# A two-mixer kernel with half of the second mixer's up and down weights decoded in the second mixer's first block

## The chip, the cores and the metric

The kernel runs on one core of a Trainium2 chip. The metric is the time of one execution on the device in microseconds (us). The engines are named as in the profile: PE (TensorE, matmuls), PEld (its weight loads), DVE (VectorE), ACT (ScalarE), POOL (GpSimd) and SP (SyncE, which issues every DMA here).

## The reference, cut to what matters

The inputs are r, k and v (4 batches, 8 heads, 768 positions, 48 channels each), the decay w and the bonus u, and the weights of two mixers. Three layers follow one another:

```python
# 1: a linear attention with a state that decays
cur = einsum('bhd,bhe->bhde', u * k[t], v[t])
y[t] = einsum('bhd,bhde->bhe', r[t], state + cur)
state = w * state + einsum('bhd,bhe->bhde', k[t], v[t])
# 2: mixer 1 (384 -> 1024 -> 384) with a convolution over 3 positions
h = maximum(x @ w_in, 0)
x = (h * sigmoid(conv3(h, conv_w))) @ w_out
# 3: mixer 2 (384 -> 1536 -> 384) with a layer norm
xn = (x - mean) / sqrt(var + 1e-6) * g_ln
out = x + maximum(xn @ w_ch1, 0) @ w_ch2
```

The weights reach the kernel as 64-bit floating-point numbers, two 32-bit words each. The kernel turns them into 32-bit numbers itself, and splits every number into a high part and a low part, so that a product is three matmuls (high by high, high by low, low by high).

## The kernel before, in words

**Tiles and blocks.** The positions are cut into 24 tiles of 128 for the attention and into 8 blocks of 384 (three tiles) for the mixers. `attn_tile` (L237) and `state_update` (L310) make one tile in two steps of the generator `attention` (L331); `step()` runs one such step. Mixer 1 (`mixer1`) runs over 8 slices f of its hidden width per block. For each f, `moe1_up` (L385) makes nine matmuls into `psm`, DVE and ACT apply the convolution and the gate (L376, L377, L382, L383, L393, L394, L396), and `down` makes nine matmuls into `acc`, two to three slices later (`LAG` is 3). Mixer 2 (`mixer2`) runs over 12 slices per block in the same way; its `moe2_up` (L402) has only one ACT operation (L409) and one DVE operation (L410) per slice. `norm` prepares the next block's normalised input. All of mixer 1's blocks, with the attention between their slices, come before all of mixer 2's blocks; the blocks' results go through DRAM in between.

**The weights.** Every weight matrix is decoded in pieces. A piece (a "job", `wjob`, L126) is one DMA into one of three buffers `st` and a generator of steps: the absolute value (ACT), a clamp, a shift and two combining operations (DVE), the high part (ACT) and the low part (DVE). A piece takes four calls of the generator, and the low part falls to the fifth, which goes on to the next piece. There are 22 pieces, in the order of `wjobs`: three of the first half of `w_in` (512 wide; all later ones but the next three of `w_in` are 768 wide), one of `w_out`, three of the second half of `w_in`, three of `w_out`, six of `w_ch1` (three for slices 0 to 5, three for slices 6 to 11), and six of `w_ch2` (two slices each). `wload(n)` issues the DMAs of the first n pieces. `wdo(n, last)` makes n steps, none beyond the piece `last`, and issues loads ahead (L190). `need(job)` makes all steps up to the end of a piece at once.

**Where the steps are placed.** `tables()` (L571) issues the first three tiles' loads and the first three pieces' loads, tile before piece. During the first four attention tiles the loop at L673 makes two steps after each `step()`, up to the last piece of the first half of `w_in`. In mixer 1 there are two slots per slice, 16 per block, and `after1` (L690) makes steps in them by these lines:

```python
            if j == 0:
                wdo(2, wo_job[NF1 - 1])
            elif j < NB - 2:
                wdo(slot[0] % 3 == 0, c1_job[NF2 - 1])
            else:
                wdo(slot[0] % 2 == 0, c2_job[4])
```

In mixer 2, `after2` (L719) makes two steps per slice, and `before2` (L715) calls `need` for the pieces that the slice reads.

**What orders the work.** The matmuls, the weight pieces' DMAs and their ACT and DVE operations are marked to be kept in program order among themselves (`pe`, `so`, `ao`, `vo`). All other instructions are placed on their engine's queue by the tile framework's scheduler, which works from program order, dependences and its own simulated times; each queue then runs in order on the chip. PSUM has two buffers for `psm`, three for `acc` and three for the attention.

Of the kernel before, what the change touches and what calls it, by code (L numbers as in the profile page):

```python
# [16 lines left out]
DM = H * D  # L17
# [4 lines left out]
NF2 = FF2 // 128  # L22
# [6 lines left out]
NB = B * BPB  # L29
NP = H // 2  # L30
PR = 112
WN = 768
# [11 lines left out]
def body(ctx, tc, r, k, v, w, u, w_in, conv_w, w_out, g_ln, w_ch1, w_ch2, out):  # L44
# [81 lines left out]
    def wjob(src, n, hi, lo, scale=None):  # L126

        st = []

        def load():  # L130
            st.append(io.tile([128, 2 * WN], I32, tag="st", name="st", bufs=3))
            dst = st[0][:, 0:2 * n]
            if len(src.shape) == 3:
                dst = dst.rearrange("p (a n) -> p a n", a=src.shape[1])
            so.dma_start(out=dst, in_=src.bitcast(I32))

        def steps():
            t = yield from decode(st[0], n)
            if len(src.shape) == 3:
                t = t.rearrange("p (a n) -> p a n", a=src.shape[1])  # L140
            kw = {} if scale is None else {"scale": gl[:, scale:scale + 1]}
            ao.activation(out=hi, in_=t, func=AF.Copy, **kw)
            yield
            if scale is None:
                vo.tensor_tensor(out=lo, in0=t, in1=hi.bitcast(F32), op=ALU.subtract)
            else:
                vo.scalar_tensor_tensor(out=lo, in0=t, scalar=kw["scale"], in1=hi.bitcast(F32),
                                        op0=ALU.mult, op1=ALU.subtract)
        wjobs.append((load, steps()))
        return len(wjobs) - 1  # L150
# [3 lines left out]
    def rows2(w_, f):  # L154
        return w_[f * 128:f * 128 + 256, :].rearrange("(a p) d -> p a d", p=128)
# [14 lines left out]
    for f0 in range(0, FF2, WN):  # L170
        for kt in range(KT):
            for f in range(f0 // 128, (f0 + WN) // 128):
                c1_job[f] = len(wjobs)
            wjob(w_ch1[kt * 128:kt * 128 + 128, f0:f0 + WN], WN, c1h[f0 // WN][kt],
                  c1l[f0 // WN][kt], kt)
    for f in range(0, NF2, 2):
        c2_job[f] = c2_job[f + 1] = wjob(rows2(w_ch2, f), 2 * DM, c2h[f // 2], c2l[f // 2])
    w_loaded, w_done = [0], [0]

    def wload(count):  # L180
# [5 lines left out]
    def wdo(count=1, last=None):  # L186

        for _ in range(count):
            while w_done[0] < (len(wjobs) if last is None else last + 1):
                wload(w_done[0] + 2)  # L190
                if next(wjobs[w_done[0]][1], "end") != "end":
                    break
                w_done[0] += 1
# [8 lines left out]
    def load_tile(n):  # L202
        if n >= NT:
            return
        b, i = divmod(n, TPB)
        sl = slice(i * C, i * C + C)
        rt = rbuf[n % 3]
        kt = io.tile([128, H, D], F32, tag="k", name="kt", bufs=3)
        vt = vbuf[n % 3]
        nc.sync.dma_start(out=kt, in_=k[b, :, sl, :].rearrange("h t d -> t h d"))  # L210
        nc.sync.dma_start(out=rt[:, :, 0:D], in_=r[b, :, sl, :].rearrange("h t d -> t h d"))
        nc.sync.dma_start(out=vt[:, :, 0:D], in_=v[b, :, sl, :].rearrange("h t d -> t h d"))
        loaded[n] = (rt, kt, vt)
# [359 lines left out]
    def tables():  # L573
        wc = ap.tile([PR, NP, 1], F32, tag="wc", name="wc", bufs=1)
        v_.memset(wc, 1.0)
        wv = w.rearrange("(p two) d -> two d p", two=2)
        for q in range(2):
            nc.sync.dma_start(out=wc[64 * q:64 * q + D], in_=wv[q].unsqueeze(2), allow_slow_non_contiguous=True)
        nc.sync.dma_start(out=tku[:, 1], in_=u.unsqueeze(0).to_broadcast([128, H, D]))
        load_tile(0)  # L580
        wload(1)
        load_tile(1)
        wload(2)
        load_tile(2)
        wload(3)
        nc.sync.dma_start(out=gl, in_=g_ln.rearrange("(k p) -> p k", p=128), allow_slow_non_contiguous=True)
        cst = ap.tile([128, 6 * NF1], I32, tag="cst", name="cst", bufs=1)
        cview = cst.rearrange("p (k f two) -> p k f two", k=3, two=2)
        for tap in range(3):
            nc.sync.dma_start(out=cview[:, tap], in_=conv_w[tap].bitcast(I32).rearrange("(f p two) -> p f two", p=128, two=2),  # L590
                              allow_slow_non_contiguous=True)
        make_identity(nc, ident)
        for t in rbuf + vbuf + [kks[:, 0, 0], kks[:, 1, 0]]:
            g_.memset(t[:, :, D:64], 0.0)

        pw = ap.tile([PR, NP, 8], F32, tag="pw", name="pw", bufs=1)
        ng = ap.tile([PR, NP, 8], F32, tag="ng", name="ng", bufs=1)
        tkd = ap.tile([PR, NP, C], F32, tag="t2", name="tkd", bufs=4)
        g_.memset(tr[:, :, 64:65], 1.0)
        v_.memset(tkd[:, :, 63:64], 1.0)  # L600
        v_.tensor_scalar(out=pw[:, :, 0:1], in0=wc, scalar1=DECAY_MIN, scalar2=DECAY_MAX, op0=ALU.max, op1=ALU.min)
        for e in range(1, 8):
            v_.tensor_tensor(out=pw[:, :, e:e + 1], in0=pw[:, :, e - 1:e], in1=pw[:, :, e - 1:e], op=ALU.mult)
        v_.reciprocal(out=ng, in_=pw)
        for e in range(7):
            m = 1 << e
            for eng, t, up, dn, o, top in ((v_, tkd, ng, pw, 63, 64), (g_, tr, pw, ng, 64, 63)):
                cnt = min(m, top - m + 1)
                if cnt > 0:
                    eng.tensor_tensor(out=t[:, :, o + m:o + m + cnt], in0=t[:, :, o:o + cnt],  # L610
                                      in1=up[:, :, e:e + 1].to_broadcast([PR, NP, cnt]), op=ALU.mult)
                bot = C - 1 - top
                cnt = min(m, bot - m + 1)
                if cnt > 0:
                    eng.tensor_tensor(out=t[:, :, o - m - cnt + 1:o - m + 1], in0=t[:, :, o - cnt + 1:o + 1],
                                      in1=dn[:, :, e:e + 1].to_broadcast([PR, NP, cnt]), op=ALU.mult)
        pt = ps_a.tile([128, NP, C], F32, tag="pa", name="ptk")
        for p in range(NP):
            pe.transpose(pt[:, p, 0:PR], tkd[:, p, :], ident[0:PR, 0:PR])
        for q in range(2):  # L620
            a_.activation(out=tku[:, 0].rearrange("x (p q) d -> x q p d", q=2)[:, q], in_=pt[:, :, 64 * q:64 * q + D],
                         func=AF.Copy)
        v_.tensor_copy(out=w128, in_=pw[:, :, 7:8])
        for t in sbd:
            g_.memset(t, 0.0)
        g_.memset(nhalf, -0.5)
        g_.memset(later, 1.0)
        g_.affine_select(out=later, in_=later, compare_op=ALU.is_gt, fill=0.0, base=0, pattern=[[0, NP], [1, C]],
                         channel_multiplier=-1)
        return cst  # L630
# [32 lines left out]
    def prefetch(j):  # L663
# [5 lines left out]
        return steps  # L669

    cst = tables()
    decayed_k(0)
    while finished[0] < EARLY - 1:  # L673
        step()
# [4 lines left out]
    for j in range(NB):  # L679
        slot = [0]  # L680
        while finished[0] < min((j + 1) * TT - (j % 2), NT - 1):
            step()

        def before1(f):
            if f < NF1:
                need(wi_job[f // 4])
            if f >= LAG - 1:
                need(wo_job[f - LAG + 1])

        def after1(f):  # L690
            slot[0] += 1
            pace[0] += 2 if j else 1.9
            if j == 1:
                pace[0] += 0.4
            if pace[0] >= 5:
                pace[0] -= 5
                step()
            if j == 0:
                wdo(2, wo_job[NF1 - 1])
            elif j < NB - 2:  # L700
                wdo(slot[0] % 3 == 0, c1_job[NF2 - 1])
            else:
                wdo(slot[0] % 2 == 0, c2_job[4])
            if j == NB - 1:
                if slot[0] == 1:
                    ahead[0] = prefetch(0)
                elif slot[0] >= 7:
                    next(ahead[0], None)

        mixer1(xT[j], spill(j), before1, after1)  # L710
# [3 lines left out]
    for j in range(NB):  # L714
        def before2(f):  # L715
            need(c1_job[f])
            need(c2_job[max(f - LAG + 1, 0)])

        def after2(f):  # L719
            wdo(2)  # L720
            if f == 1 and j + 1 < NB:
                ahead[0] = prefetch(j + 1)
            elif f >= 4:
                next(ahead[0], None)

        b, s0 = divmod(j, BPB)
        x1s, xn = normed.pop(j)
        mixer2(xn, lambda acc, x1s=x1s, b=b, s0=s0: finish(
            acc, x1s, lambda t0: out[b, s0 * T + t0:s0 * T + t0 + 128, :]), before2, after2)
        for _ in ahead[0]:  # L730
            pass
# [34 lines left out]
```

## Time and profile before

| what | value |
|---|---|
| three runs, median (lowest to highest) | 686.56 us (684.76 to 686.9) |
| the profiled execution's own time | 685.54 us |
| its span, first to last instruction | 683.8 us |
| mean granted share of TensorE's clock | 0.974 |
| busy: PE, PEld, DVE, ACT, POOL | 639.0, 609.8, 435.1, 270.1, 95.0 us |

The profile is of one execution. Its times begin at the span's start; 1.74 us of the profiled execution's time lie around the span. In a view of waits, a row says which engine and line waited for which, with the total, the count and the longest. In a timeline a row has its start, its duration, the engine, the line, the operation, what it writes and reads, and the idle time before it with what ended it. By the starts of L393 (64 of them) and L409 (96), mixer 1's block 0 begins at about 44.5 us, its block 1 at 104.8, block 6 at 308.6, mixer 2's block 0 at 366.0 and its block 1 at 402.8.

### The profile page before, as it was taken

Reading aid. Unit: us, or ns where it says so; the run is one execution under the profiler, and the core shown is the slowest. Engines: PE = TensorE matmul, PEld = TensorE weight load, DVE = VectorE, ACT = ScalarE, POOL = GpSimd, SP = SyncE. Lnnn points to the kernel's source line nnn. Section 1 sums busy time; section 2 is a strip of 40 time slices with the busy share of each in tenths; the row PEclk is TensorE's granted clock in tenths of the full one; section 3 lists DMA queues with packets and bytes.
Section 4 is the critical chain, followed back from the end, with each engine's and each line's share of the span. In section 5 each row is a group of like instructions: output and inputs, shape, how many; then the busy total and the mean of one; then the engine's idle time right before and its main releaser. Section 6 shows DMA issues by size and latency. Waiting matters only on the chain.

```text
span 683.8 us, 12373 instructions
## 1 busy us (share of the span) xinstructions
PE 639.0 (93%) x5100; PEld 609.8 (89%) x5100; DVE 435.1 (64%) x822; ACT 270.1 (39%) x537; POOL 95.0 (14%) x137
## 2 busy tenths in 40 slices
PE   3874799999999999999999999999999999999996
PEld 3764698889989978999999999999999999999995
DVE  5989899998988888997998524142332415242211
ACT  1336456556565565657675312122121212112110
POOL 6342032221212222200110000000000000000000
PEclk9887699999999999999999999999999999999999
DMA  8953542343324241403301002020201102020101
GB/s 180 180 133 78 154 107 72 86 104 82 94 71 95 57 119 22 140 1 114 130 36 59 23 1 70 1 70 1 70 1 36 34 1 70 1 69 1 35 1 39
DMA packets 93842, 45.15 MB, mean 66 GB/s; under 512 B 80337, under 2 KB 89682, under 8 KB 93778
## 3 DMA queue, kind: packets, MB, share of 16 engines
q1 hardware_dynamic: 93778, 44.28, 24.8%
q8 instruction: 42, 0.69, 0.4%
q14 instruction: 22, 0.18, 0.1%
HBM read 34.83 MB, written 9.44 MB: 65 GB/s over the span
## 4 chain that ended last, share of the span: by engine, by line
PE 54%; DVE 34%; ACT 5%; issue 3%; DMA 2%; POOL 1%; SPq 0%; ACTq 0%; DVEq 0%; POOLq 0%
PE acc L70 25%; PE psm L70 25%; DVE c L396 9%; DVE wdec L70 6%; DVE aT L271 3%; DVE gl L383 3%; DVE c L377 3%; DVE kks L224 2%; ACT c L376 1%; DVE rT L248 1%; DVE sn L325 1%; ACT c L394 1%; DVE xl L295 1%; PE pxt L70 1%; POOL av L256 1%
## 5 line engine op out<-in xcount | busy, mean ns | idle before, releaser
L410 DVE SCALAR_TENSOR_TENSOR rl<-psm,rh 128x384 fp32r<-128x384 f32 x96 | 53.3, 555 | 143.2 <-ACT rh L409 143.2
L409 ACT ACTIVATE rh<-psm 128x384 fp32r<-128x384 f32 x96 | 47.2, 491 | 212.2 <-PE psm L70 212.2
L70 PE MATMUL psm<-xnh,c1h 128*128 128x384 f32 x288 | 98.8, 343 | 0.0
L70 PE MATMUL psm<-xnh,c1l 128*128 128x384 f32 x288 | 97.5, 339 | 0.0
L70 PE MATMUL acc<-c2h,rh 128*128 128x384 f32 x288 | 97.2, 338 | 0.0
L70 PE MATMUL acc<-c2h,rl 128*128 128x384 f32 x288 | 97.2, 338 | 0.0
L70 PE MATMUL acc<-c2l,rh 128*128 128x384 f32 x288 | 97.1, 337 | 0.0
L70 PE MATMUL psm<-xnl,c1h 128*128 128x384 f32 x288 | 96.9, 336 | 0.0
L396 DVE SCALAR_TENSOR_TENSOR c<-h,cw,c 128x384 f32<-128x384 f32 x128 | 86.7, 681 | 12.0 <-ACT c L394 11.5
L70 PE MATMUL psm<-xh,wih 128*128 128x386 f32 x192 | 69.5, 362 | 8.2 <-ACT wih L70 4.7
L70 PE MATMUL acc<-woh,gh 128*128 128x384 f32 x192 | 68.2, 355 | 8.2 <-ACT woh L70 7.5
L70 PE MATMUL acc<-woh,gl 128*128 128x384 f32 x192 | 66.2, 345 | 2.0 <-DVE gl L383 1.9
L70 PE MATMUL acc<-wol,gh 128*128 128x384 f32 x192 | 65.9, 343 | 1.3 <-DVE wol L70 1.3
L70 PE MATMUL psm<-xl,wih 128*128 128x386 f32 x192 | 66.9, 348 | 0.0
L70 PE MATMUL psm<-xh,wil 128*128 128x386 f32 x192 | 66.7, 347 | 0.1
L433 POOL TENSOR_TENSOR rs<-rs,nhalf 128x1 f32<-128x1 f32 x24 | 15.6, 664 | 306.2 <-DVE rs L432 306.0
L70 PEld LDWEIGHTS psm<-xnl,c1h 128*128 128x128 f32 x288 | 54.3, 189 | 0.0
L70 PEld LDWEIGHTS psm<-xnh,c1h 128*128 128x128 f32 x288 | 54.3, 189 | 0.0
L70 PEld LDWEIGHTS psm<-xnh,c1l 128*128 128x128 f32 x288 | 54.2, 188 | 0.0
L70 PEld LDWEIGHTS acc<-c2l,rh 128*128 128x128 f32 x288 | 54.1, 188 | 0.0
L70 PEld LDWEIGHTS acc<-c2h,rh 128*128 128x128 f32 x288 | 54.1, 188 | 0.0
L70 PEld LDWEIGHTS acc<-c2h,rl 128*128 128x128 f32 x288 | 54.0, 188 | 0.0
(103 smaller groups left out, 1122.8 us busy)
## 6 DMA issues: line engine op xcount, KB each, us to landing
st<-in_moe_w_ch_dram SPq DMA_DIRECT2D x12, 768.0 KB, 5.3
rvbuf<-in_r_dram SPq DMA_DIRECT2D x24, 192.0 KB, 3.1
kt<-in_k_dram SPq DMA_DIRECT2D x24, 192.0 KB, 3.4
rvbuf<-in_v_dram SPq DMA_DIRECT2D x24, 192.0 KB, 3.1
x_dram<-x SPq DMA_DIRECT2D x24, 192.0 KB, 1.9
x1b<-x_dram SPq DMA_DIRECT2D x24, 192.0 KB, 2.9
out_dram<-x1b SPq DMA_DIRECT2D x24, 192.0 KB, 1.9
st<-in_moe_w_in_dram SPq DMA_DIRECT2D x6, 512.0 KB, 5.2
```

The source lines that it names most:

```text
L70: return lambda *args, **kw: tc.keep_in_program_order(op(*args, **kw))
L224: v_.tensor_tensor(out=kks[:, n % 2, :, :, 0:D], in0=loaded[n][1].unsqueeze(1).to_broadcast([128, 2, H, D]), in1=tku, op=ALU.mult)
L248: v_.tensor_tensor(out=rT, in0=prt[0:PR], in1=tr, op=ALU.mult)
L256: g_.tensor_tensor(out=av, in0=kks[:, n % 2, 1, :, 0:D], in1=rt[:, :, 0:D], op=ALU.mult)
L271: v_.copy_predicated(out=aT[:, q], mask=later.bitcast(I32), data=dps[q])
L295: v_.tensor_tensor(out=xl[:, :, sl], in0=yps, in1=xh[:, :, sl].bitcast(F32), op=ALU.subtract)
L377: v_.tensor_tensor(out=st["c"], in0=st["h"][:, 1:T + 1], in1=st["c"], op=ALU.mult)
L383: v_.tensor_tensor(out=st["gl"], in0=st["c"], in1=st["gh"].bitcast(F32), op=ALU.subtract)
L396: v_.scalar_tensor_tensor(out=c, in0=h[:, o:o + T], scalar=cw[:, tap, f:f + 1], in1=c, op0=ALU.mult, op1=ALU.add)
L409: a_.activation(out=gh, in_=ps[:, 0:T], func=AF.Relu)
L410: v_.scalar_tensor_tensor(out=gl_, in0=ps[:, 0:T], scalar=0.0, in1=gh.bitcast(F32), op0=ALU.max, op1=ALU.subtract)
L433: g_.tensor_tensor(out=rs[:, 1:2], in0=rs[:, 0:1], in1=nhalf, op=ALU.pow)
```

## The change

The pieces of `w_ch1` and `w_ch2` are put in another order: three of `w_ch1` (slices 0 to 5), three of `w_ch2` (slices 0 to 5), and then the same for slices 6 to 11. The first six of these twelve pieces are decoded in mixer 1's blocks 2 to 7 (none in block 1), the last six in mixer 2's first block, three steps per slice. Loads are issued three pieces ahead of the finished ones instead of two. The first piece's load comes right after the first tile's k, and three of its steps are made before the first `decayed_k`.

```diff
                 c1_job[f] = len(wjobs)
             wjob(w_ch1[kt * 128:kt * 128 + 128, f0:f0 + WN], WN, c1h[f0 // WN][kt],
                   c1l[f0 // WN][kt], kt)
-    for f in range(0, NF2, 2):
-        c2_job[f] = c2_job[f + 1] = wjob(rows2(w_ch2, f), 2 * DM, c2h[f // 2], c2l[f // 2])
+        for f in range(f0 // 128, (f0 + WN) // 128, 2):
+            c2_job[f] = c2_job[f + 1] = wjob(rows2(w_ch2, f), 2 * DM, c2h[f // 2], c2l[f // 2])
...
-                wload(w_done[0] + 2)
+                wload(w_done[0] + 3)
...
         nc.sync.dma_start(out=kt, in_=k[b, :, sl, :].rearrange("h t d -> t h d"))
+        if n == 0:
+            wload(1)
...
         load_tile(0)
-        wload(1)
         load_tile(1)
...
     cst = tables()
+    wdo(3)
     decayed_k(0)
...
             if j == 0:
                 wdo(2, wo_job[NF1 - 1])
-            elif j < NB - 2:
-                wdo(slot[0] % 3 == 0, c1_job[NF2 - 1])
-            else:
-                wdo(slot[0] % 2 == 0, c2_job[4])
+            elif j > 1:
+                wdo(slot[0] % 3 != 0 if j >= NB - 2 else slot[0] % 8 == 0, c2_job[NF2 // 2 - 1])
...
         def after2(f):
-            wdo(2)
+            wdo(3)
```

## Rows read from the trace of the kernel before

**Rows 1.** The page, parts 1 and 2: busy time by engine; TensorE's clock by slice.
```profile
PE 639.0 (93%) x5100; PEld 609.8 (89%) x5100; DVE 435.1 (64%) x822; ACT 270.1 (39%) x537; POOL 95.0 (14%) x137
...
PEclk9887699999999999999999999999999999999999
```
**Rows 2.** Windows by stage: length, PE, PEld, DVE, ACT, POOL busy, PEclk, DMA share, GB/s.
```profile
0.00:17.00 17.00, 6.36 (x46) 5.27 (x47) 9.24 (x33) 2.43 (x4) 11.77 (x39) 1.00 0.88 179
17.00:44.50 27.50, 21.16 (x344) 17.67 (x342) 25.52 (x45) 10.91 (x23) 12.26 (x15) 0.86 0.86 174
44.50:104.80 60.30, 45.86 (x387) 40.41 (x389) 54.81 (x91) 31.57 (x57) 11.64 (x10) 0.78 0.42 114
104.80:308.60 203.80, 199.10 (x2175) 182.77 (x2174) 184.91 (x314) 120.99 (x248) 43.70 (x50) 1.00 0.32 77
308.60:366.00 57.40, 55.43 (x360) 53.70 (x359) 51.67 (x107) 40.83 (x82) 5.75 (x6) 1.00 0.24 83
366.00:402.80 36.80, 36.80 (x215) 36.69 (x215) 21.04 (x38) 13.24 (x26) 0.00 (x0) 1.00 0.12 38
402.80:441.60 38.80, 38.80 (x227) 38.70 (x226) 13.01 (x30) 7.38 (x16) 1.65 (x3) 1.00 0.10 31
```
**Rows 3.** The same windows for decoding alone (tile wdec): length, DVE, ACT busy, PEclk, DMA.
```profile
44.50:104.80 60.30, 25.81 (x39) 10.62 (x14) 0.78 0.42 114
104.80:308.60 203.80, 24.84 (x31) 11.05 (x12) 1.00 0.32 77
308.60:366.00 57.40, 11.83 (x15) 5.21 (x6) 1.00 0.24 83
366.00:402.80 36.80, 11.83 (x15) 5.12 (x6) 1.00 0.12 38
```
**Rows 4.** PE's waits in 44.5 to 104.8 (two rows), in 104.8 to 308.6 (one).
```profile
PE acc L70 <- ACT woh L70: 7.5, 1, 7.5
PE psm L70 <- ACT wih L70: 4.7, 2, 2.5
...
PE prt L70 <- DVE aT L271: 1.5, 3, 0.7
```
**Rows 5.** Timeline of the start: first weight piece, first decayed keys, last decay table.
```profile
7.24 1.70 DVE L610 TENSOR_TENSOR tkd<-tkd,ng 112x4 f32<-112x4 f32 x7
...
8.99 1.13 SPq L70 DMA_DIRECT2D st<-in_moe_w_in_dram  x1
...
10.68 1.83 DVE L224 TENSOR_TENSOR kks<-kt,tku 128x768 f32<-128x768 f32 x2 [1.75 <-ACT tku L621]
...
19.25 0.68 ACT L70 ACTIVATE wdec<-st 128x512 f32<-128x512 f32 x1
...
19.97 1.66 DVE L70 TENSOR_SCALAR wdec<-wdec 128x512 f32<-128x512 f32 x2
...
23.26 0.67 DVE L70 SCALAR_TENSOR_TENSOR wdec<-st,wdec 128x512 int32<-128x512 int32 x1
```
**Rows 6.** SP's own waits: its weight loads behind the buffers that DVE frees.
```profile
SPq L70 <- DVE wdec L70: 26.9, 6, 9.0
```
**Rows 7.** The page, part 6: the second mixer's weight loads, median us to landing.
```profile
st<-in_moe_w_ch_dram SPq DMA_DIRECT2D x12, 768.0 KB, 5.3
```
**Rows 8.** Timelines of ACT and DVE in mixer 2's first block.
```profile
366.41 0.90 ACT L70 ACTIVATE wdec<-st 128x768 f32<-128x768 f32 x1
...
383.25 0.49 ACT L409 ACTIVATE rh<-psm 128x384 fp32r<-128x384 f32 x1 [1.14 <-PE psm L70]
...
385.34 0.96 DVE L70 TENSOR_TENSOR c2l<-wdec,c2h 128x768 fp32r<-128x768 f32 x1 [0.45 <-ACT c2h L70]
```
**Rows 9.** Lines of DVE, 366.0 to 402.8: busy, mean ns; idle before them.
```profile
L410 DVE SCALAR_TENSOR_TENSOR rl<-psm,rh 128x384 fp32r<-128x384 f32 x12 | 6.6, 551 | 9.2 <-ACT rh L409 9.2
...
L70 DVE TENSOR_TENSOR c2l<-wdec,c2h 128x768 fp32r<-128x768 f32 x3 | 2.9, 958 | 2.6 <-ACT c2h L70 2.6
```

## The prediction, made before the changed kernel was run

> **What bounds the kernel now.** I read the page's busy times first, then the granted clock by slice, then a table of windows by stage, then the same table for the decode alone, then waits and timelines where a stage loses time. The page says that PE is busy for 93% of the span, and the clock is below full speed only in the first slices [rows 1]. So the loss lies early, and the windows show where [rows 2]. From 402.8 us on, a block of mixer 2 is pure PE: 38.8 of 38.8 us busy, DVE at 13.0. Nothing can be won there but fewer matmuls. From 104.8 to 308.6 (mixer 1's blocks 1 to 5, with attention) PE is busy 199.1 of 203.8 us, DVE 184.9 of 203.8: PE bounds it and DVE stands close behind. What PE still waits for there is the end of a DVE operation (the attention mask, 1.5 us in three waits) [rows 4]. From 44.5 to 104.8 (block 0) PE is busy for 45.9 of 60.3 us at a granted clock of 0.78, DVE for 54.8: here DVE sets the pace, and PE stands still for weights that are not decoded, 7.5 us for the first down piece and 4.7 us in two waits for up pieces [rows 2, 4]. From 17 to 44.5 DVE is busy 25.5 of 27.5 us; before 17 us it is busy for only 9.2 [rows 2].
>
> **The sum** is made against the profiled execution, 685.54 us, which is 1.02 us below the median of 686.56. Each term is a difference in us.
>
> **Start: -2.0.** Three steps of the first piece move from the saturated stretch behind 17 us to a place before the first decayed keys. In the trace these are two DVE operations of together 1.66 us and one of 0.67, and 0.68 us on ACT [rows 5]; 2.3 us of DVE work. DVE has 7.8 us idle before 17 us [rows 2], of which 1.75 us lie directly before the first decayed keys, while DVE waits for ACT [rows 5]. If the weight has landed by then the work is covered, and everything behind it, which DVE paces, comes 2.3 us earlier; I take 2.0. The piece's load was issued at 8.99 us [rows 5]; right behind the first keys it goes out some 6 us earlier. Its 512 KB at 179 GB/s, the rate of that window [rows 2], hold up the loads queued behind it (the first r and v, the second tile) by 2.9 us. That is covered, since the first decayed keys wait for ACT and not for a load. If DVE's queue instead holds the clamp ahead of the keys before the piece is there, the start is late by the wait: a piece that lands at 14 us starts the keys at about 16.3 instead of 10.7, 5.6 late, of which the 2.3 us of work done come back. Ends: -5 (PE's waits in block 0 shrink too) and +5.
>
> The Trainium skill, DMA: Bandwidth & Descriptors, section on queues, rings and completion order, says that each DMA engine consumes a ring's descriptors in order, which speaks against putting a large load ahead of small urgent ones. By it this term would be as much as 2.9 us worse, -2.0 becoming about +1.
>
> **Block 0: 0.** Its 25.8 us of decode on DVE [rows 3] stay; the same two steps per slot. Its PE stalls follow DVE and shift with it. Loads come one piece earlier; they were not what PE waited for [rows 4]. Ends -5 and +3: a stall that falls differently also changes how long the clock stays low.
>
> **Blocks 1 to 5: -5.0.** Six pieces are decoded there now, 24.8 us of DVE and 11.1 of ACT [rows 3]. After the change block 1 has none and blocks 2 to 5 have two slots of sixteen each, eight steps, which is two pieces, 8.3 us. DVE is relieved of 16.6 us, from 184.9 to 168.3 of 203.8. PE can give back at most what it loses: 203.8 less 199.1 is 4.7 us [rows 2], perhaps twice that, as matmul ends are modelled. I take 5.0, since the waits named are for DVE [rows 4] and DVE then has a sixth of the time free. Ends 0 and -9.
>
> The Trainium skill, Perfetto Trace Analysis, section on the most-contended engine, judges TensorE by its weight loads and not by its matmuls. Weight loads fill 182.8 of these 203.8 us, DVE 184.9 [rows 2], so it names no clear bound; read as PE-bound throughout, it would put this term at 0 (rival 1).
>
> **Blocks 6 and 7: +1.5.** Today three pieces, 11.8 us of DVE [rows 3]. After it, two slots in three: eleven steps in block 6 and the rest of the 24 early in block 7, together sixteen steps, four pieces: 3.9 us more. DVE has 5.7 of 57.4 us idle and PE 2.0 [rows 2]. If the idle time covers it the cost is 0; if DVE is the bound it is 3.9. With 97% of DVE taken, I put it between, nearer the lower end.
>
> **Mixer 2's first block: +1.5.** Here six pieces instead of three: another 11.8 us on DVE, from 21.0 to 32.9 of 36.8 us [rows 2, 3], plus part of the second block's norm, which is now done earlier. ACT gets 5.1 more on 13.2: covered. The point is order. The seventh slice needs the second half of the up weights, three pieces. Its `rh` starts at 383.25, so its matmuls start near 381.6. In the trace three pieces begun at 366.41 end at 386.30 [rows 8], at two steps per slice. At that pace PE would stall about 3.5 us (the last third of the weights is needed near 382.8). At three steps per slice the pieces can run as fast as their chain: 3.95 us of DVE each and some 0.9 us of waiting for ACT's high part (2.6 us for three) [rows 9], with 0.7 us for the `rl` of 1.3 slices: about 5.6 us each, 16.8 in all, just in time. If all of it queues ahead of `rl` and the norm, the three pieces (11.9), seven `rl` (3.9), the waits (2.6) and 5 us of other DVE work (the window's 21.0 less 11.8 of decode and 6.6 of `rl` leave 2.6; I double it, as the second block's norm slides in) make 23.4 us against 16.8, a stall of 6.6. I take 1.5, ends 0 and +6.6. The last three pieces are needed two slices and more later and are covered.
>
> **Loads three ahead: 0.** There are three buffers, so a load now waits for the buffer of the piece just finished. SP already stands 26.9 us behind such buffers [rows 6]; queued behind it are tile loads and the blocks' stores and reloads. In mixer 2's first block a piece takes 1.3 slices, some 4.2 us, less than the 5.3 us of a load [rows 7], so two ahead would have been tight there and three cover it. No stall of PE in the trace names a load of weights.
>
> Sum: -2.0 + 0 - 5.0 + 1.5 + 1.5 = -4.0, 681.5 for the profiled execution, 682.5 against the median.
>
> **Rivals.** *1. No change* (about 686.5, 684.5 to 688.6): PE is the bound of blocks 1 to 5, its 4.7 us come back only by a fraction, and what is won there and at the start (together 3) is paid in blocks 6 and 7 and in mixer 2 (3). For it: PE at 98% in that window; against it: the waits name DVE.
>
> *2. Slower* (about 691.5): DVE comes out of block 7 with work left over, and the seventh slice of mixer 2's first block waits the full 6.6 us for its up weights. A stall of PE of that length has a second price: after the 7.5 us stall of block 0 the clock's slice falls to 0.6 [rows 1], and 17 us at 0.6 are up to 6.7 us; I take 4 for one. -2.0 - 5.0 + 1.5 + 6.6 + 4 = +5.1. It decides from a stall of some 4 us on, if the clock falls with it (+2.5 in all). For it: DVE at 97% in blocks 6 and 7 and more than half of its 36.8 us added to afterwards [rows 2, 3]; against it: three steps per slice give the chain time, and the scheduler can put a slice's needs first.
>
> *3. Faster by more* (676): block 0's stalls shorten enough that the clock stays at 2.4 GHz. Today it is granted 0.78 there [rows 2], and the slices after the 7.5 us stall show 0.6 [rows 1]. 60.3 us at 0.78 hold 13 us of lost clock; if half of it comes back, -6 more. The Trainium skill, TensorE: Matmul & The Clock Gate, part 1, has the engine throttled by default and released by activity, which would do just this; the trace agrees in that the clock fell after the stall.
>
> **Chances.** Forecast 0.52, rival 1 0.20, rival 2 0.15, rival 3 0.13. The forecast's own range is 678.5 to 685.5. The whole range, 675 to 691, takes in rivals 1 and 3 and nearly half of rival 2. About 0.3% (2.1 us) is what a measurement here tells from no change: faster than 684.5 has 0.13 and most of the forecast's 0.52, 0.57; within it 0.22; slower 0.21, rival 2 with the bad ends of the start and of block 0.
>
> **What would show it.** Right: first decode operation before the first decayed keys and block 0 some 2 us earlier; the window of blocks 1 to 5 near 199 us with DVE near 168; DVE almost full from block 6 to the end of mixer 2's first block, PE's wait for the seventh slice under 2 us. Wrong: DVE waiting at its queue's head for the first weight; PE idle of several us on `c1h` or `c1l`; blocks 1 to 5 unchanged in length with DVE down.

## The result, and the profile after

The changed kernel takes 690.94 us (median of six runs, 689.61 to 692.93) beside 686.73 for the kernel before: a ratio of 1.0065, 95% interval 1.0045 to 1.0086. It is slower by 4.2 us where 4.0 us faster was forecast. The profiled execution took 690.66 us, span 688.9, so its stages may be set against the 683.8 of before.

Of the page of the changed kernel, parts 1 and 2, to be set beside [rows 1]:

```profile
PE 635.6 (92%) x5100; PEld 607.5 (88%) x5100; DVE 442.0 (64%) x822; ACT 270.0 (39%) x537; POOL 91.7 (13%) x137
...
PEclk9998599999999999999999999999999999999999
```

The busy times say next to nothing: PE is busy for less time than before, and the span is 5.1 us longer. The windows by stage show it (columns as in [rows 2]), cut at the same events (block 0 at its first up matmul, 44.55 before and 45.68 after; its first L393 comes 3 to 4 us later):

```profile
0.00:17.00 17.00, 6.31 (x46) 5.23 (x47) 10.66 (x34) 2.98 (x5) 12.30 (x39) 1.00 0.87 176
17.00:45.60 28.60, 19.00 (x344) 14.85 (x342) 25.96 (x43) 10.16 (x22) 11.30 (x16) 0.99 1.00 182
45.60:105.70 60.10, 44.57 (x383) 39.58 (x383) 54.70 (x92) 32.09 (x57) 10.04 (x11) 0.81 0.40 109
105.70:303.60 197.90, 196.65 (x2171) 182.34 (x2172) 172.79 (x290) 114.44 (x239) 43.12 (x50) 1.00 0.29 67
303.60:362.70 59.10, 55.79 (x364) 54.27 (x363) 54.93 (x104) 41.63 (x85) 2.66 (x3) 1.00 0.25 84
362.70:407.70 45.00, 39.31 (x216) 38.23 (x215) 34.83 (x64) 18.57 (x32) 2.34 (x3) 0.96 0.25 79
407.70:446.50 38.80, 38.80 (x227) 38.69 (x226) 13.09 (x30) 7.36 (x16) 1.65 (x3) 1.00 0.09 31
```

Length against length, after less before: start +1.1, block 0 -0.2, blocks 1 to 5 -5.9, blocks 6 and 7 +1.7, mixer 2's first block +8.2, everything behind it +0.2. The sum is +5.1, the difference of the spans. One block gives back more than the five blocks won. The decode alone (tile `wdec`, columns as in [rows 3]) moved as it was meant to: 30 operations on DVE in mixer 2's first block are six pieces of five.

```profile
105.70:303.60 197.90, 7.00 (x9) 3.68 (x4) 1.00 0.29 67
303.60:362.70 59.10, 16.66 (x21) 6.98 (x8) 1.00 0.25 84
362.70:407.70 45.00, 23.63 (x30) 10.35 (x12) 0.96 0.25 79
```

What PE waited for in mixer 2's first block (the view of waits):

```profile
PE psm L70 <- ACT c1h L70: 3.6, 1, 3.6
PE pxt L70 <- DVE xn L437: 1.7, 1, 1.7
PE psm L70 <- DVE c1l L70: 0.4, 1, 0.4
```

The same place in PE's timeline, the block's seventh slice:

```profile
379.77 0.55 PE L70 MATMUL pxt<-ident,xn 128*128 128x128 f32 x3 [1.68 <-DVE xn L437]
...
381.03 0.34 PE L70 MATMUL psm<-xnh,c1l 128*128 128x384 f32 x1
384.94 0.45 PE L70 MATMUL psm<-xnh,c1h 128*128 128x384 f32 x1 [3.57 <-ACT c1h L70]
...
386.27 0.34 PE L70 MATMUL acc<-c2h,rh 128*128 128x384 f32 x1
...
387.36 0.53 PE L70 MATMUL acc<-c2l,rh 128*128 128x384 f32 x1
...
389.46 0.62 PE L70 MATMUL psm<-xnh,c1h 128*128 128x384 f32 x1
389.92 0.34 PE L70 MATMUL psm<-xnl,c1h 128*128 128x384 f32 x1
```

Six of the slice's nine matmuls run, and then the queue stands until the third up piece's high part is there; the `acc` matmuls behind, whose weights have long been decoded, start only after the slice, at 386.27. Ahead of the slice stand the transposes of the next block's norm, which wait too. The three waits make 5.7 us. Behind the stall a matmul takes 0.53 us instead of 0.34: the granted clock is 0.50 from 386.5 to 389.9 us, the 1.2 GHz level, and full again behind. From 386.44 to 389.46 us PE does what takes about 1.6 us at full clock (an estimate, by starts 0.17 to 0.18 us apart before the stall), so that is another 1.4. Together 7.1 of the 8.2 us.

And why the third piece was late, in the timelines of ACT (the first line) and DVE (the others):

```profile
363.07 0.89 ACT L70 ACTIVATE wdec<-st 128x768 f32<-128x768 f32 x1
...
364.75 0.54 DVE L70 TENSOR_SCALAR wdec<-wdec 128x768 f32<-128x768 f32 x1
...
370.05 1.02 DVE L70 SCALAR_TENSOR_TENSOR c1l<-wdec,gl,c1h 128x768 fp32r<-128x768 f32 x1 [1.01 <-ACT c1h L70]
370.98 0.55 DVE L70 TENSOR_SCALAR wdec<-wdec 128x768 f32<-128x768 f32 x1
...
374.75 0.56 DVE L432 BATCH_NORM_STATS2 bs<-x1b 128x6 f32<-128x384 f32 x1 [1.29 <-DMA x1b<-x_dram]
...
378.25 1.01 DVE L70 SCALAR_TENSOR_TENSOR c1l<-wdec,gl,c1h 128x768 fp32r<-128x768 f32 x1
...
384.92 1.02 DVE L70 SCALAR_TENSOR_TENSOR c1l<-wdec,gl,c1h 128x768 fp32r<-128x768 f32 x1 [1.00 <-ACT c1h L70]
```

The first clamp comes 2.0 us into the block, and from it to the end of the third low part it is 21.2 us. The second piece alone takes 8.3, because the norm of the next block stands among its steps, and the norm's first operation holds DVE's queue for 1.29 us until its input has been reloaded.

### The profile page after: what moved, and what is told of

It reads as the page before. It is cut to its first block, busy times and chain, and to the rows that moved or that the text cites. A ratio compares the mean times of both kernels' runs of the same rounds, so it can differ in the third digit from the quotient of the medians.

```text
span 688.9 us, 12373 instructions
## 1 busy us (share of the span) xinstructions
PE 635.6 (92%) x5100; PEld 607.5 (88%) x5100; DVE 442.0 (64%) x822; ACT 270.0 (39%) x537; POOL 91.7 (13%) x137
## 4 chain that ended last, share of the span: by engine, by line
PE 75%; DVE 17%; issue 2%; ACT 2%; DMA 2%; POOL 1%; SPq 0%; DVEq 0%; POOLq 0%; ACTq 0%
PE acc L70 33%; PE psm L70 32%; DVE wdec L70 3%; DVE c L398 3%; PE yps L70 3%; PE dps L70 2%; DVE aT L273 2%; DVE c L379 1%; PE prt L70 1%; PE pxt L70 1%; DVE gl L385 1%; DVE kks L226 1%; PE pst L70 1%; PE pkt L70 1%; POOL av L258 1%
## 5 line engine op out<-in xcount | busy, mean ns | idle before, releaser
L398 DVE SCALAR_TENSOR_TENSOR c<-h,cw,c 128x384 f32<-128x384 f32 x128 | 85.2, 668 | 13.3 <-ACT c L396 12.4
L378 ACT ACTIVATE c<-c 128x384 f32<-128x384 f32 x64 | 33.6, 525 | 58.2 <-DVE c L398 58.1
```

What stands on the lines that cost most here:

```text
L378: a_.activation(out=st["c"], in_=st["c"], func=AF.Sigmoid)
L398: v_.scalar_tensor_tensor(out=c, in0=h[:, o:o + T], scalar=cw[:, tap, f:f + 1], in1=c, op0=ALU.mult, op1=ALU.add)
```

## The experiments

All kernels below but four (the up pieces first and their repeat, the norm later, and five up pieces in mixer 1) halve `GC`, the loop length of the general path, which isn't run with these inputs; that makes room in SBUF. No run halves it alone. The changed kernel and the kernel with one piece more, which halves it, have the same order of work on PE, ACT, DVE and POOL up to about 350 us, where the added steps begin; what halving does to the time is not measured. Ratios are to the kernel before on the same chip, with 95% intervals.

**Start alone, move alone, loads alone.** The start alone is the kernel before with these lines:

```diff
+        if n == 0:
+            wload(1)
...
-        wload(1)
...
+    wdo(3)
     decayed_k(0)
```

> The kernel before with the start of the change alone: the first piece's load right behind the first keys, and three steps before the first decayed keys. Theory (the start costs): in the changed kernel the first 45 us became 1.1 us longer, since the three early steps run beside POOL's work, take longer there and stand in front of the first attention mask on DVE. Then block 0 begins at 45 to 46 us instead of 44.5, and the time is 687 to 688.5 against 686.7 (ratio 1.001 to 1.003). Rival (the start gains, and what was lost there came from the loads three ahead, which filled the DMA engines): block 0 begins at 42 to 43 us, the time is 684.5 to 685.5 (ratio 0.997 to 0.998).

684.76 us, 0.9970 (0.9959 to 0.9981). Both halves came out, against each other: block 0 begins at 45.3 us, 0.8 later, as the theory has it, and the kernel is faster all the same, as the rival has it. The gain lies behind block 0 (mixer 2's first block begins at 363.9 instead of 366.0), where no edited line acts, though the scheduler has put DVE's and ACT's work there in another order; its profiled execution, 685.14 us, is also its slowest run. The place of the cost is confirmed by the timeline of the start in the changed kernel:

```profile
14.52 2.77 POOL L263 TENSOR_SCALAR_AFFINE_SELECT aT<-a 128x1024 f32<-128x1024 f32 x2
...
15.23 2.61 DVE L70 SCALAR_TENSOR_TENSOR wdec<-st,wdec 128x512 int32<-128x512 int32 x2
...
17.76 1.32 DVE L273 COPY_PREDICATED aT<-later,dps 128x512 f32<-128x512 int32 x2
```

Two operations of which one takes 0.67 us in [rows 5] take 2.61 together beside a busy POOL, and the first attention mask stands behind them (in the start alone 2.60, and the mask at 17.56). In the kernel before the mask began at 15.72:

```profile
15.72 1.35 DVE L271 COPY_PREDICATED aT<-later,dps 128x512 f32<-128x512 int32 x2 [0.81 <-PE dps L70]
```

The move alone is the rest of the change without the loads:

```diff
+        for f in range(f0 // 128, (f0 + WN) // 128, 2):
...
+            elif j > 1:
+                wdo(slot[0] % 3 != 0 if j >= NB - 2 else slot[0] % 8 == 0, c2_job[NF2 // 2 - 1])
...
-            wdo(2)
+            wdo(3)
```

> The kernel before with the move alone: the new order of pieces, six of them decoded in mixer 1 and six in mixer 2's first block at three steps per slice; loads two ahead, start as before. Theory (the move makes the loss): blocks 1 to 5 take 198 us instead of 204, blocks 6 and 7 59 instead of 57.4, mixer 2's first block 45 instead of 36.8: +3.5 to +4.5 in all, 690 to 691 (ratio 1.005 to 1.007). Rival (the stall in mixer 2's first block comes of the loads three ahead, which hold up the reload of the next block's input on SP's queue): the first block is under 40 us and the time is about 684 to 685.

688.96 us, 1.0042 (1.0028 to 1.0055). Blocks 1 to 5 take 198.5 us, blocks 6 and 7 61.1, mixer 2's first block 41.5, with PE waiting 3.1 us for the third up piece's high part and 0.4 for its low part. The move makes the gain and the loss, and the rival's time falls; but the loss is smaller than the theory's 45 us block, and the time is 1 us below its range. One thing is as the rival has it: the place of the second block's norm. Its first operation on DVE (L430, L432 in the change) starts at 343.1 us in the kernel before and at 356.5 here, in block 7, but at 374.75 in the change, among the up pieces. In every kernel here with the move and loads three ahead that norm stands in mixer 2's first block, in every one with the move and loads two ahead in block 7.

```diff
-                wload(w_done[0] + 2)
+                wload(w_done[0] + 3)
```

> The kernel before with the loads three pieces ahead alone. Theory (free): no stage of the trace waits for a weight load, so every stage keeps its length; 686 to 687 against 686.5 (ratio 0.999 to 1.001). Rival (the loads, earlier by one piece, fill the DMA engines during the first attention tiles and delay their r, k and v): block 0 begins 1 us or more after 44.5, 687.5 to 688.5 (ratio 1.0015 to 1.003).

684.27 us, 0.9976 (0.9966 to 0.9986): faster than either expected. Every stage boundary of its profile lies within 1.1 us of the kernel before, so the profile doesn't show where 1.6 us went. PE's and POOL's work is in the order of the kernel before, and DVE's and ACT's differs only between about 325 and 372 us. On the kernel before the loads ahead cost nothing.

**Is it the deadline or the amount?** The changed kernel with the pieces in the old order, so that all six up pieces fall into mixer 1:

```diff
-        for f in range(f0 // 128, (f0 + WN) // 128, 2):
-            c2_job[f] = c2_job[f + 1] = wjob(rows2(w_ch2, f), 2 * DM, c2h[f // 2], c2l[f // 2])
+    for f in range(0, NF2, 2):
+        c2_job[f] = c2_job[f + 1] = wjob(rows2(w_ch2, f), 2 * DM, c2h[f // 2], c2l[f // 2])
...
-                wdo(slot[0] % 3 != 0 if j >= NB - 2 else slot[0] % 8 == 0, c2_job[NF2 // 2 - 1])
+                wdo(slot[0] % 3 != 0 if j >= NB - 2 else slot[0] % 8 == 0, c1_job[NF2 - 1])
...
-            need(c2_job[max(f - LAG + 1, 0)])
+            if f >= LAG - 1:
+                need(c2_job[f - LAG + 1])
```

> The changed kernel with the pieces in the old order: all six up pieces in mixer 1, all six down pieces in mixer 2's first block, each needed two slices apart, from the fourth slice on. The same number of steps in the same slots. Theory (a deadline: the seventh slice waits for three up pieces at once): the stall at the seventh slice goes, the first block takes 37 to 39 us instead of 45, the time is 683 to 685.5 against 686.7 (ratio 0.994 to 0.998). Rival (an amount: DVE cannot do six pieces and a norm in that block in whatever order): the block stays at 43 us or more with PE waiting for down pieces, the time is 689 to 691.

683.04 us, 0.9953 (0.9937 to 0.9970). Its windows of blocks 1 to 5, blocks 6 and 7 and mixer 2's first block:

```profile
105.40:303.40 198.00, 196.71 (x2171) 182.40 (x2172) 172.92 (x291) 114.57 (x240) 42.56 (x50) 1.00 0.28 67
303.40:361.60 58.20, 55.23 (x357) 53.09 (x356) 54.91 (x104) 41.83 (x86) 3.36 (x3) 1.00 0.26 86
361.60:400.00 38.40, 38.39 (x222) 37.86 (x222) 33.79 (x63) 17.92 (x31) 2.52 (x3) 1.00 0.28 93
```

Six pieces are decoded in the block as in the change, though six down pieces here, and the norm stands among them too (from 372.60). DVE does 33.8 us of work in it instead of 34.8, and the block takes 38.4 us instead of 45.0 with PE never idle. DVE was busy for only 77% of the block that stalled and for 88% of the one that doesn't. It is the deadline.

The changed kernel with one piece more in mixer 1:

```diff
-                wdo(slot[0] % 3 != 0 if j >= NB - 2 else slot[0] % 8 == 0, c2_job[NF2 // 2 - 1])
+                wdo(slot[0] % 3 != 0 if j >= NB - 2 else slot[0] % 8 == 0, c2_job[NF2 // 2 - 1] + 1)
```

> The changed kernel with one piece more in mixer 1: the first of the three up pieces for slices 6 to 11 is decoded there, in slots that are free in block 7; two up pieces are left before the seventh slice. Theory (deadline: three pieces of about 6 us each, begun behind the first slice, end some 3 to 5 us after the seventh slice wants them): two pieces end 2 us ahead, the stall and the fall of the clock go, mixer 2's first block takes 37 to 39 us instead of 45; blocks 6 and 7 take 0 to 2 us more than 59; the time is 683 to 686 (ratio 0.995 to 0.999). Rival (amount of work on DVE in that block and before it): DVE has the same work in the two stretches together, the loss moves into block 7, the time is 688 to 690.

685.1 us, 0.9988 (0.9976 to 1.0000). The first block takes 37.5 us, blocks 6 and 7 60.9: theory, including the price in block 7. In mixer 2's first block PE no longer waits for any weight; the transposes still wait for the norm:

```profile
PE pxt L70 <- DVE xn L437: 2.3, 1, 2.3
```

The changed kernel with the norm of the second block later:

```diff
-            if f == 1 and j + 1 < NB:
+            if f == (6 if j == 0 else 1) and j + 1 < NB:
...
-            elif f >= 4:
+            elif f >= (7 if j == 0 else 4):
```

> The changed kernel with the norm of the second block begun at the seventh slice of mixer 2's first block instead of the second (the reload too), so that none of it stands among the up pieces. Deadline theory with the norm as its larger part: the third up piece ends some 5 us earlier, the first block takes 39 to 41 us instead of 45, the time is 686 to 688 (ratio 0.999 to 1.002). Rival (the chain of the three pieces alone sets it): the block shrinks by less than 2 us, the time is 689 to 691.

689.51 us, 1.0056 (1.0035 to 1.0077): the rival's time, with 2.2 us off the block (42.8), a little more than the rival has. Without a norm among them, the three up pieces take 18.7 us from the first clamp instead of 21.2 and still end late: PE waits 2.6 and 0.4 us for them. The norm made the miss larger; it didn't make it.

**Room for more?** The next three start from the kernel with the up pieces first (683.0).

```diff
-                wdo(slot[0] % 3 != 0 if j >= NB - 2 else slot[0] % 8 == 0, c1_job[NF2 - 1])
+                wdo(slot[0] % (2 if j >= NB - 2 else 4) == 0, c1_job[NF2 - 1])
```

> The kernel with all up pieces in mixer 1 (683.0), with a step in every fourth slot of blocks 2 to 5 and every second of blocks 6 and 7 instead of every eighth and two in three: two more pieces in the middle, two fewer at the end. Theory (DVE bounds blocks 6 and 7, and has room in blocks 2 to 5, where it is busy for 172.9 of 198 us and PE for 196.7): blocks 6 and 7 take 57 us instead of 58.2, blocks 1 to 5 stay at 198 to 199: 681.5 to 682.5 (ratio 0.992 to 0.994). Rival (every us of decode in blocks 2 to 5 costs PE as in the kernel before, where 24.8 us cost 5.8): 8 us more cost 2, the time is 683.5 to 685 (ratio 0.995 to 0.998).

684.35 us, 0.9972 (0.9956 to 0.9988): the rival's time. Blocks 1 to 5 take 204.0 us with 15.8 us of decode, as long as before with 24.8; blocks 6 and 7 drop to 55.3. That the decode alone costs these 6 us isn't shown, since the window's granted clock is 0.98 and not 1.00:

```profile
103.50:307.50 204.00, 200.74 (x2173) 186.23 (x2174) 179.76 (x300) 118.57 (x244) 43.82 (x50) 0.98 0.30 73
```

The clock fell twice in it (0.92 from 103.5 to 125 us, 0.93 from 200 to 225). The first fall lies in block 1, which has no steps in either kernel and takes 41.6 us instead of 40.0; blocks 2 to 5 take 162.5 instead of 158.0, the second fall among them. The ten executions differ in the same way: the four with a mean granted clock of 0.981 took 681.96 to 683.66 us, three of them the theory's time, the six with 0.972 to 0.977 took 684.21 to 685.63.

```diff
-    wdo(3)
     decayed_k(0)
```

> The kernel with all up pieces in mixer 1 (683.0), without the three steps before the first decayed keys; the first piece's load stays early. Theory (the three steps stand in front of the first attention mask and cost about 1 us at the start): block 0 begins at 44.3 to 44.8 us instead of 45.5, the time is 682 to 682.5 (ratio to the kernel before 0.993 to 0.995). Rival (they gain, as the start alone made the kernel before 0.3% faster): block 0 begins later than 45.5, or a later stage grows, and the time is 684 to 685 (ratio 0.996 to 0.998).

684.36 us, 0.9976 (0.9966 to 0.9986): the rival's time. Block 0 begins at 45.1 us rather than 45.5, and mixer 2's first block ends at 401.1 instead of 400.0.

```diff
+            if f0 > 0 and kt == KT - 1:
+                down_piece(0)
...
-    for f in range(0, NF2, 2):
-        c2_job[f] = c2_job[f + 1] = wjob(rows2(w_ch2, f), 2 * DM, c2h[f // 2], c2l[f // 2])
+    for f in range(2, NF2, 2):
+        down_piece(f)
...
-                wdo(slot[0] % 3 != 0 if j >= NB - 2 else slot[0] % 8 == 0, c1_job[NF2 - 1])
+                wdo(slot[0] % 3 != 0 if j >= NB - 2 else slot[0] % 8 == 0, c2_job[0] - 1)
```

(`down_piece(f)` makes the piece of `w_ch2` for slices f and f + 1 by the line that stood in the loop.)

> The kernel with the up pieces first, with five of them in mixer 1 and the sixth behind the first down piece in mixer 2's first block. Theory (deadline: two pieces of about 6 us end some 13 us after the block's first slice, the sixth up piece is wanted at 18 to 19): no stall at the seventh slice; blocks 6 and 7 take 55 to 57 us instead of 58.2, the first block 38.4 to 41 (seven pieces fill DVE); 681.5 to 684.5. Rival (amount: seven pieces and a norm are more than DVE can do in that block): the first block takes over 42 us, PE waits for down pieces, 685 to 688.

694.74 us, 1.0117 (1.0101 to 1.0133), worse than either expected. Blocks 6 and 7 take 59.4 us, mixer 2's first block 48.6, and PE's longest wait is now for a down piece:

```profile
PE acc L70 <- ACT c2h L70: 6.7, 1, 6.7
```

The second down piece is third in the queue (its low part starts at 384.07 us, as the third up piece's did at 384.92 in the change), but due earlier: PE stands for it from 377.4 us, 15.2 us into the block, and in the change for the third up piece only from 381.4, 18.7 us into it. DVE is busy for 30.9 of the 40 us from 372 on: again a deadline. The granted clock is 0.87 in these 40 us, so part of the loss is the clock's.

**What holds up.** The kernel with the up pieces first once more; the same slots, `need` and three steps per slice on the kernel before, with its own start and loads two ahead; and that with the changed start.

> The kernel with all up pieces in mixer 1 (the start and the loads three ahead as in the change) once more, with more rounds, since four runs of it stood against runs of 0.25% up and down. Theory (the deadline was the whole loss of the change): ratio to the kernel before 0.994 to 0.997, some 682.5 to 684. Rival (it was a lucky set of runs, and it is worth no more than the start alone): 0.997 to 0.999.

682.85 us, 0.9952 (0.9935 to 0.9968), the same as the first time.

> The kernel before with the up pieces first in mixer 1 and the down pieces in mixer 2's first block alone: start as before, loads two ahead. Theory (the move with the deadline met is what pays, 5.9 us in blocks 1 to 5 less some 2.4 later): 682.5 to 684 (ratio 0.994 to 0.9975). Rival (two loads ahead come late for pieces of three steps per slice, 4.2 us each against 5 us to landing): mixer 2's first block shows DVE or ACT waiting for the pieces, over 40 us instead of 38.4, 685 to 686.

684.14 us, 0.9964 (0.9950 to 0.9977); the first block takes 37.4 us with loads two ahead, so they don't come late there. Blocks 6 and 7 take 61.6.

> The same with the changed start too, loads still two ahead. Theory (start and move add up: the start alone measured 0.3%): 681 to 683 (ratio 0.991 to 0.995). Rival (what the start alone gave came from another order of DVE's work in blocks 1 to 7, which the move changes anyway): the same as without it within 0.15%.

683.2 us, 0.9957 (0.9941 to 0.9972), 0.07% from the one without the start: the rival. Start and move don't add up. Of the 0.48% gained over the kernel before, the kernel with the move alone, its deadline met, has 0.36; what lies between the two ratios is within their intervals.

## Why the prediction was wrong

The sum missed by 9.1 us, of which 6.7 lie in mixer 2's first block and 3.1 at the start.

**Start, -2.0: wrong sign, +1.1.** The steps did move ahead of 17 us, the first decayed keys did not come later (10.73 us instead of 10.68), and DVE's queue never stood for the first piece. What failed is "the work is covered". DVE's idle time there lies in front of the first attention mask, which came 2.0 us later, and beside POOL's long operations, where two of the moved steps took twice their time; that POOL is the cause is not isolated. A delay of the loads behind the early piece is not seen at the first tile: r's first transposes began at 9.90 us, before at 9.86. But with the early load, the loads three ahead and no steps, block 0 still began 0.5 us later than in the kernel before, so the loads may have a part of the 1.1. By the Trainium skill's rule on a ring's order (DMA: Bandwidth & Descriptors, section on queues, rings and completion order) this term was to become about +1, near the +1.1 measured; but at the first tile the trace shows none of the delay that this price stands on.

**Block 0, 0: right,** -0.2. **Blocks 1 to 5, -5.0: right,** -5.9, with DVE at 172.8 of 197.9 us and PE's recorded idle time down from 4.7 to 1.3. The stage is 198 to 199 us long in every profile here with 7 to 8 us of decode in it, so less decode on DVE did it; which waits of PE it shortened is shown only in part, as the idle time accounts for 3.4 of the 5.9. (The waits named before were not all for DVE: one of 1.2 us was for ACT.) DVE was relieved of 12.1 us and not 16.6: the decode fell by 17.8, but DVE's other operations took 5.7 more, which no run explains. Rival 1 falls: it had the 4.7 us come back by a fraction only, and 5.9 came back. The Trainium skill (Perfetto Trace Analysis, section on the most-contended engine) judges TensorE's headroom by its weight loads or its share of peak, and not by its matmuls' busy time; the trace agrees, since weight loads filled 182.8 of 203.8 us and so left room for the 5.9, which the matmuls' 199.1 did not.

**Blocks 6 and 7, +1.5: right,** +1.7.

**Loads three ahead, 0: right in size on the kernel before, and not without effect with the move,** where the norm of the second block goes with them into mixer 2's first block. It cost that block, and took work out of block 7: the move alone has 61.1 and 41.5 us in blocks 6 and 7 and in that block, the change 59.1 and 45.0.

**Mixer 2's first block, +1.5: this term made the prediction wrong; +8.2.** The mechanism was named, the seventh slice waiting for three up pieces, and its price mis-sized. I put three pieces at "about 5.6 us each, 16.8 in all, just in time". They began 2.0 us into the block, while the 16.8 counts from its start, and took 21.2 from there. The estimate had an `rl` per slice in it, but not the norm of the next block (that stands only in its worst end, +6.6), nor the norm's wait of 1.29 us at the head of DVE's queue. The norm is 2.5 to 3.4 of it: the three pieces took 18.7 us with the norm later and 17.8 in the move alone, where it stands in block 7. Even so they missed the slice by 3.0 and 3.5 us. The three pieces of the kernel before, 386.30 less 366.41 [rows 8], showed 19.9 us, counted from the first absolute value on ACT; counted so, the change's took 22.9. Taken as it stands that row gave a stall of 3.5, and it was set aside for an estimate; it would have been nearer, but with the other terms unchanged the sum would still have been faster, -2.0. The second price came with the stall: the clock fell, 1.4 us, as rival 2 said.

**Rival 2** (given 0.15) is what happened in mixer 2's first block, but its total, 691.5 beside the 690.94 measured, is near by luck. Its start was 3.1 us too low and its clock 2.6 us too high (4 instead of 1.4), which nearly cancel; the stall was 5.7 us instead of 6.6. Nor did DVE come out of block 7 with work left over: the block's 30 decode operations are those of its own six pieces.

At the stall matmuls take 0.34 us before it, 0.53 from 386.72 us on and 0.34 again at 389.92. The Trainium skill's rule on the clock (TensorE: Matmul & The Clock Gate, part 1: throttled by default, released by activity) agrees with that. Block 0 kept its low clock (0.81 against 0.78), so rival 3 did not happen. In the stage before it the clock did rise, from 0.86 to 0.99, and the stage was 1.1 us longer all the same, with DVE busy for 26.0 of 28.6 us: a higher clock gave nothing where DVE sets the pace.

**What is open.** Start alone and loads alone are each 0.24 to 0.30% faster than the kernel before, though block 0 begins later in both. Both also halve `GC`, so neither gain can be put down to its edited lines. On top of the move with its deadline met, start and loads together (and an unhalved `GC`) add 0.12% (0.9964 to 0.9952), within the intervals; yet without the three early steps, and with `GC` halved, that kernel lost 0.23% (0.9953 to 0.9976). What the start is worth, and whether an order of DVE's queue or `GC` does it, was not isolated.

## What to carry to other kernels

Work that is moved to where an engine is idle has to be timed by its latest start and its chain, not by the engine's free share: DVE had a quarter of the block free and PE still stood, because three serial pieces were due at one instant. Order such pieces so that each is due a step after the last; here the old order of the pieces, with as many left for the block, turned +0.65% into -0.48%. A duration that the trace shows for the same sequence of work (19.9 us for three pieces) is to be taken over an estimate from its parts, and is still no bound: a norm that moved in among the pieces made it 22.9.

## What the runs showed that was not expected

Behind a stall of 5.7 us, in three parts, the granted clock fell once, at 1.4 us; it fell as well behind the 3.5 us of the move alone and the 3.0 with the norm later. Two pieces more in blocks 2 to 5, with DVE at 87% there, went with 6 us more in blocks 1 to 5, in a profile in which the clock fell twice in them; how much of that is the decode is open. In the kernels with the move, loading weights one piece earlier went with a norm in a later stage. And a change that moves stage boundaries by no more than 1.1 us in the profile, the loads three ahead (with `GC` halved), moved the median by 1.6 us over ten runs.
